# A table of the order of 3662 operations: positions 1075 to 2195 set anew, and 29 maxima tied to VectorE

## The chip, the cores and the metric

The kernel runs on one core of a Trainium2 chip. The metric is the device time of one execution in microseconds (us). The kernel before was run three times: 1040.69, 1041.87 and 1043.01 us, median 1041.87.

## What is computed

Two layers in one kernel, all in fp32:

```python
# linear attention: batch 8, heads 8, 576 positions, head 64, 128 features
proj = x @ w_phi;  proj -= max(abs(proj));  phi = [exp(proj), exp(-proj)]
kv = phi(k).T @ v;  z = sum(phi(k));  num = phi(q) @ kv;  den = phi(q) @ z + 1e-6
x = (num / den) as 4608 tokens x 512
# two dense layers over the tokens
h = x @ w_in                       # 512 -> 2048
g = 0.5 * h * (1 + erf(h / sqrt(2)))
out = g @ w_out                    # 2048 -> 512
```

## The kernel before

**Attention** goes batch by batch (b = 0 to 7), four pairs of heads each. For keys, `k_unit` projects a unit into one PSUM bank ("pp", tile `pk_...`) on TensorE; VectorE takes the row maxima (`mx`) and subtracts them out of the bank into `ek` (or `er` for the last 64 positions, the "rest"); ScalarE makes both exponents; TensorE then multiplies with the values (`kv_...`). `ek` and `er` have two buffers each, one per sign, so the subtraction of a unit writes where the kv product of an earlier unit reads. For queries, `q_front` projects into the same bank (`pq_...`), ScalarE copies it to `pc`, GpSimd takes the maximum over the partitions (`mb`, line 399), VectorE subtracts, ScalarE makes the exponents (`ef`), TensorE forms the numerators (`pn_...`). From batch 3 on the denominators are formed by VectorE (lines 457 and 460) and a sum over the partitions on GpSimd (`db`, line 410); they go through DRAM (`d_d`, `dc`, `r_d`) as reciprocals.

**The dense layers** take 18 blocks of 256 tokens. In blocks 0 to 7 (`block`) there are eight units: "first products" (`up`, into `ph`: 2 x 12 matmuls, each operand split into two fp32r parts `xh`, `xl`), two Gelus on ScalarE (`gh`, and `ph` in place), the difference `gl` on VectorE, and "second products" into `po` (2 x 6 matmuls). Blocks 8 to 17 (`seven`) use seven products of half blocks into `pa` and `pb`; they need sums of the weights `w_out`, which VectorE makes early (`ts`), which are stored in DRAM (`t_d`), and which `fetch_sums` loads into `tw_0` to `tw_7` and back into halves of `w_o0` to `w_o15`. The tw tiles lie where attention's tiles lay, so their loads wait until attention has ended.

**What sets the order.** Each engine runs its instructions in program order. The program is written as a list of operations with their dependencies, and `Plan.order` emits them in the order of the table `ORDER`, 3662 numbers. An operation that comes early for one engine holds up what stands behind it on that engine alone. All DMAs of this kernel but two go through SyncE's queue, which also runs in order. A second table, `TOGETHER`, holds pairs n:m: the GpSimd operation n gets a wait for the VectorE operation that stands just ahead of operation m, so that the reduction begins when VectorE begins m, which reads PSUM:

```python
if o.n in beside:
    ahead[o.n] = last
...
if o.n in together:
    self.tc.add_manual_dep(ins.ins, ahead[together[o.n]].ins.name, ...)
```

A second product's last matmul is cut in two halves of 256 columns where a first product follows (`cut` in `block`).

Of the kernel before, what the change touches and what calls it, by code (L numbers as in the profile page):

```python
# [883 lines left out]
773 1684 1689 1531 1535 807 1532 1680 838 1536 1685 839 822 844 1533 845 846 770 823 808 1741 1537 1539 1538 1540 1541 756 849 1686 1542 809 1690 1543  # L884
857 1544 1742 1545 850 1546 1547 1691 1548 810 1695 1549 811 1687 1692 851 824 840 1803 812 774 1696 919 852 1550 1551 1554 1552 1555 853 1556 1702
813 847 1553 1557 1703 814 825 1693 1697 771 818 1558 1698 1559 1804 854 815 914 1560 796 804 816 1694 826 827 1704 1699 1709 873 915 754 1705 916
1561 828 1564 1700 1565 1701 829 1562 1805 1710 858 1706 830 1566 1567 1716 1806 817 831 1717 917 859 1711 832 1707 1563 819 1708 1712 834 1569 1570
1571 874 893 1568 1574 1572 1809 1718 1575 1573 1719 1713 1576 875 644 1720 1812 860 1723 1577 1714 848 1579 861 1580 923 924 1724 925 1715 1578 876
918 1743 1581 1721 921 1582 920 1584 757 1722 1813 862 1807 926 1585 1583 863 864 855 877 1586 927 1587 865 1589 878 833 931 856 835 1588 1808 820 866
867 928 1590 1725 1726 1047 1591 836 1727 775 870 932 1750 1814 922 1810 1744 879 929 868 1592 933 971 880 1594 1751 1728 871 934 1595 1596 1597 1593  # L890
935 939 1599 1811 1745 1746 881 758 1729 882 894 886 1600 883 1601 936 869 1602 895 1815 1598 887 955 1603 1747 975 1752 1753 1730 1731 1732 1754 896
884 976 897 1604 1733 977 1757 1609 937 1764 898 978 1816 1605 872 900 1610 899 1748 1606 1749 1611 1755 973 1765 979 972 1607 885 1758 1756 901 940
1612 906 902 1759 1608 776 1766 980 1614 1760 1615 1767 907 941 1613 903 1761 1619 1616 1771 1620 1762 1772 956 1621 889 1817 1617 1763 904 1818 957
1618 930 777 1768 1773 905 942 1622 1624 1625 1626 1819 943 1623 1774 1775 1627 1629 944 778 1628 981 1630 908 1778 983 1769 1785 890 1631 945 984 985
1770 1776 1777 986 958 946 974 1779 1632 1633 1634 1635 1048 1636 1820 1639 987 952 988 1637 1640 991 888 1786 1638 1780 947 1781 1641 1782 1881 1787
1792 948 949 1644 1645 1882 938 1783 953 1642 1788 1049 1646 1784 989 1181 1053 1793 959 1050 950 954 960 1789 1821 1790 1647 1054 961 982 1643 1791
1822 1794 1649 990 1650 1651 1648 1795 962 963 1652 1883 1796 1823 964 992 993 1654 1051 891 968 1655 1057 1885 1653 1058 1884 1824 1797 909 1828 1825
1007 994 1052 995 1656 996 1059 1060 1657 1886 1835 997 951 965 1829 969 1798 1055 1887 910 966 1888 1799 1061 1836 1065 1830 1831 1658 1801 1004 1005
1832 1066 1105 998 1062 1889 1950 1826 1827 1833 999 1027 1837 1000 1056 967 1063 1064 1838 1001 1842 892 1002 1843 1067 1834 1068 1006 1069 1839 1844
1070 1109 1800 1106 1840 1951 1107 1845 1952 1953 1849 911 1071 1956 1846 1850 1959 1960 1802 1841 1110 1111 1851 1072 1008 970 1961 1962 1847 1848  # L900
1852 1853 1854 1112 1003 1113 1009 1073 912 1855 1010 1856 1028 1114 1029 1089 1011 1012 1030 1117 1108 1115 1116 1013 1857 1118 1187 1031 1863 1858
1014 1119 1864 1015 1859 1016 1032 1020 1860 1017 1865 1018 1182 1861 1183 1866 1021 1867 1862 1022 1870 1033 1871 1120 1034 1868 1019 1954 1035 1872
1036 1869 1023 1037 1873 1040 1121 1874 1875 1955 1024 1025 1026 1041 1876 1042 1038 1890 1877 1879 1957 1878 1880 1891 1039 1897 1892 1958 1898 1893
1894 1043 1122 1899 1900 1963 1901 1044 1045 1895 1046 1123 1184 1188 1124 1185 1964 1896 1186 1904 1911 1965 1912 1966 1967 1905 2028 1074 1906 1902
1125 1075 2029 1903 1907 1076 1908 1090 1913 1914 2030 1918 1915 1091 1141 1191 1077 2031 1919 1189 1192 1078 1092 1193 1909 1079 1910 1194 1080 1093
1916 1195 1081 1920 1917 1082 1083 1925 1921 1084 1922 1926 1923 1094 1086 1927 1196 1087 1085 1928 1088 1095 1929 1126 1190 1924 1161 1197 1096 1198
1127 1097 1102 1098 1128 1199 1103 1104 1932 1099 1239 1200 1100 1933 1201 1930 1934 1931 1935 1936 1939 1129 1937 1130 1101 1938 1940 1131 1202 1132
1142 2032 1133 1203 1134 1138 1207 1143 1135 1136 1941 1243 1204 1942 1241 1244 1139 2033 1140 1943 1944 1205 1240 1245 1206 1246 1945 1144 1137 1968
1946 2034 1948 1975 1947 1247 1949 2035 1976 1145 1969 2036 1146 1147 2121 1162 1248 1970 1148 1223 1149 1150 2122 1977 1151 1978 1154 1242 1152 1163
1971 1249 1972 1250 1251 2123 1155 1979 1156 1973 1252 2124 1253 1974 1254 1980 1164 2127 1153 1981 1255 1982 1165 1157 1166 1989 1167 1168 1169 1990  # L910
1158 1170 1159 1171 1983 1160 1208 1984 1174 1259 1209 1172 1256 1175 1210 1991 1176 1992 1985 1173 1224 1257 1986 1258 1993 1996 1225 1275 1177 1211
1997 1212 1226 2003 2004 1178 1213 1179 1180 1987 1214 1227 1988 1215 1228 1216 1994 1998 1217 1995 1218 1999 1220 2000 2005 2006 2007 2001 1221 1229
1222 2002 2010 1230 1219 1231 1232 2017 1233 2018 1234 2011 2008 2012 2125 1236 2013 2014 1260 1237 1235 1238 2126 2037 1261 1295 1262 2038 2009 2015
2019 2020 2128 1263 2016 2021 1264 1276 2129 2022 1277 2039 2023 1278 2044 2024 2130 2026 2025 2040 2045 2027 2041 2131 2051 2046 1279 2047 1265 2052
2132 2048 2042 2275 1280 1266 2058 1267 2099 1268 1269 2276 2059 1270 2043 2277 2049 2053 2102 2050 2105 2054 2278 2055 1272 2060 2108 2061 2062 1271
1296 1281 2056 2057 2111 1297 1282 1273 1298 2065 1274 2114 1283 1284 2072 1299 1285 1300 2073 1286 2066 2063 2067 1288 2117 2068 2069 2064 1289 1302
1290 1287 1301 2079 2120 2080 2074 1303 1291 1304 2070 1305 2075 2076 2071 2098 1292 2086 1293 2081 2101 1294 2082 2083 2087 1306 2133 2279 1307 1308
2134 1309 1310 2077 2280 1311 2078 2104 2084 2088 2107 2089 2090 2085 2110 2149 2113 2281 2150 1312 2282 1313 2283 1314 2091 2426 2092 2116 2097 2135
2106 2100 2118 2109 2115 2103 2112 2136 2137 2165 2093 2119 2095 2094 2427 2138 2096 2166 2139 2142 2140 2143 2151 2181 2152 2141 2144 2182 2153 2154
2145 2155 2158 2146 2156 2159 2157 2147 2167 2160 2168 2148 2169 2229 2170 2171 2174 2230 2172 2175 2173 2183 2176 2161 2185 2245 2246 2162 2163 2184  # L920
2186 2164 2187 2197 2190 2188 2191 2189 2213 2192 2214 2198 2177 2199 2430 2201 2178 2179 2200 2202 2180 2203 2193 2206 2204 2194 2207 2215 2195 2205
2216 2208 2196 2284 2428 2217 2218 2219 2300 2222 2220 2223 2231 2221 2301 2224 2233 2431 2316 2429 2317 2285 2209 2225 2432 2210 2226 2232 2433 2234
2211 2235 2238 2227 2236 2434 2247 2212 2228 2248 2332 2237 2239 2577 2240 2249 2241 2250 2242 2251 2254 2243 2252 2580 2255 2253 2244 2286 2256 2257
2287 2288 2258 2261 2262 2265 2259 2289 2266 2581 2263 2290 2264 2260 2267 2333 2268 2269 2270 2271 2348 2272 2273 2582 2291 2274 2293 2292 2294 2302
2349 2295 2303 2304 2305 2364 2306 2309 2307 2583 2310 2308 2365 2318 2311 2320 2380 2381 2296 2312 2297 2313 2319 2321 2298 2322 2325 2314 2323 2326
2334 2299 2315 2335 2328 2324 2327 2329 2336 2330 2337 2331 2338 2396 2341 2339 2342 2340 2350 2343 2344 2351 2352 2345 2353 2346 2354 2357 2347 2355
2435 2358 2366 2367 2356 2360 2359 2368 2361 2369 2362 2370 2373 2363 2371 2436 2374 2372 2382 2375 2383 2384 2376 2385 2377 2386 2389 2378 2387 2390
2388 2379 2451 2391 2392 2393 2394 2395 2452 2397 2467 2398 2578 2399 2400 2401 2483 2402 2405 2403 2484 2406 2437 2579 2438 2404 2408 2407 2439 2409
2412 2413 2416 2410 2440 2417 2414 2584 2441 2415 2411 2418 2468 2419 2420 2421 2422 2499 2423 2424 2442 2425 2444 2443 2445 2453 2500 2446 2454 2455
# [86 lines left out]
```

## Time and profile before

| | us |
|---|---|
| median of three runs | 1041.87 |
| lowest, highest run | 1040.69, 1043.01 |
| the profiled execution | 1041.06 |
| its span, first to last instruction | 1039.3 |
| TensorE busy | 1017.9 |
| VectorE busy | 676.3 |
| ScalarE busy | 605.5 |
| GpSimd busy | 274.8 |

The engines are PE (TensorE, matmuls), PEld (its weight loads, which overlap), DVE (VectorE), ACT (ScalarE), POOL (GpSimd) and SP (SyncE, here the DMA queue). The chain of waits follows the work that ended last back to what released it. "Idle before" is the time an engine sat idle in front of an instruction. [...]

### The profile page before, as it was taken

The numbers are of one execution on the slowest core, as the hardware profiler recorded it, in microseconds if no ns is written. First come the engines' busy times: TensorE is split into PE (matmuls) and PEld (weight loads), VectorE is DVE, ScalarE is ACT, GpSimd is POOL, SyncE is SP. The second block draws the span as 40 slices with busy tenths as digits, with TensorE's granted clock in tenths as the row PEclk, the third lists the DMA queues.
The fourth block names the chain that finished last, engine by engine and source line by source line (L and its number), as shares of the span: only waits on it lengthen the run. The fifth ranks groups of instructions, "written<-read, shape, count | busy, mean of one in ns | idle before, by whom it ended". The sixth has DMA issues, their size and how long they took to land.

```text
span 1039.3 us, 24208 instructions
## 1 busy us (share of the span) xinstructions
PE 1017.9 (98%) x10090; PEld 893.0 (86%) x10090; DVE 676.3 (65%) x1209; ACT 605.5 (58%) x1009; POOL 274.8 (26%) x72
## 2 busy tenths in 40 slices
PE   6979999999999999999999999999999999999998
PEld 5646768788878888887887889999999999999998
DVE  7899999898897875426543424565465546464655
ACT  5989888766877675757764643343343334244433
POOL 1433232544455344416566430000000000000000
PEclk9999999999999999999999999999999999999999
DMA  8765655435335343132321338201201111110000
GB/s 296 228 202 176 204 196 156 144 95 174 116 104 185 116 126 115 58 83 74 92 76 47 94 111 319 46 28 42 55 29 41 42 42 42 42 41 19 24 22 21
DMA packets 87325, 107.10 MB, mean 103 GB/s; under 512 B 29020, under 2 KB 57244, under 8 KB 87216
## 3 DMA queue, kind: packets, MB, share of 16 engines
q1 hardware_dynamic: 86928, 105.30, 32.9%
q8 instruction: 79, 1.29, 0.5%
q10 hardware_dynamic: 288, 0.26, 0.1%
q14 instruction: 30, 0.25, 0.1%
HBM read 75.87 MB, written 29.66 MB: 102 GB/s over the span
## 4 chain that ended last, share of the span: by engine, by line
PE 92%; DVE 2%; ACT 2%; DMA 2%; issue 1%; SPq 0%; DVEq 0%; ACTq 0%
PE ph L220 38%; PE po L220 18%; PE pa L220 10%; PE pb L220 7%; PE pn L220 5%; PE kv L220 5%; PE pq L220 3%; PE pk L220 3%; PE dn L220 1%; PE pn_rest L220 1%; DMA kt<-in_kT_dram 1%; ACT ek L330 1%; DMA qt<-in_qT_dram 1%; DVE ob L261 0%; ACT ef L404 0%
## 5 line engine op out<-in xcount | busy, mean ns | idle before, releaser
L220 PE MATMUL ph<-xh,w_i 128*128 128x256 f32 x2304 | 417.6, 278 | 0.0
L220 PEld LDWEIGHTS ph<-xh,w_i 128*128 128x128 f32 x2304 | 357.3, 188 | 9.1 <-issue 3.8
L220 PE MATMUL ph<-xl,w_i 128*128 128x256 f32 x1152 | 318.6, 277 | 0.0
L220 PEld LDWEIGHTS ph<-xl,w_i 128*128 128x128 f32 x1152 | 216.4, 188 | 0.2
L399 POOL PARTITION_ALL_REDUCE mb<-pc x36 | 119.6, 3321 | 205.8 <-ACT pc L255 112.4
L220 PE MATMUL po<-w_o,gh 128*128 128x512 f32 (+1 forms) x518 | 161.9, 395 | 0.0
L410 POOL PARTITION_ALL_REDUCE db<-pc x20 | 124.4, 6221 | 90.1 <-DVE pc L460 82.0
L261 DVE TENSOR_TENSOR sg<-ga 128x256 f32<-128x256 f32 (+1 forms) x240 | 84.5, 376 | 63.2 <-ACT ga L699 59.9
L220 PEld LDWEIGHTS po<-w_o,gh 128*128 128x128 f32 x518 | 91.8, 188 | 27.4 <-issue 4.7
L220 PE MATMUL pa<-w_o,oh 128*128 128x256 f32 x640 | 112.9, 276 | 0.2 <-DVE ob L261 0.2
L220 PE MATMUL po<-w_o,gl 128*128 128x512 f32 (+1 forms) x296 | 101.1, 363 | 0.0
L699 ACT ACTIVATE ga<-ph 128x512 f32<-128x512 f32 x80 | 47.8, 598 | 90.3 <-PE ph L220 62.4
L261 DVE TENSOR_TENSOR gl<-ph,gh 128x512 fp32r<-128x512 f32 x64 | 43.7, 685 | 84.5 <-ACT ph L610 84.4
L220 PEld LDWEIGHTS pa<-w_o,oh 128*128 128x128 f32 x640 | 96.5, 188 | 0.4 <-DVE ob L261 0.4
L220 PE MATMUL pa<-w_o,ol 128*128 128x256 f32 x320 | 88.4, 276 | 0.0
L261 DVE TENSOR_TENSOR ul<-sg,uh 128x384 fp32r<-128x384 f32 x80 | 44.6, 558 | 67.0 <-ACT uh L255 65.7
L220 PE MATMUL pb<-tw,uh 128*128 128x256 f32 x464 | 83.3, 277 | 0.7 <-DVE ob L261 0.5
L330 ACT ACTIVATE ek<-ek 128x1024 f32<-128x1024 f32 x64 | 67.6, 1057 | 12.6 <-DVE ek L261 10.7
L609 ACT ACTIVATE gh<-ph 128x512 fp32r<-128x512 f32 x64 | 38.2, 598 | 58.8 <-PE ph L220 31.5
L404 ACT ACTIVATE ef<-pc 128x1024 f32<-128x1024 f32 (+1 forms) x72 | 68.1, 972 | 6.8 <-DVE pc L261 6.3
L220 PE MATMUL pn<-ef,kvn 128*64 128x512 f32 (+1 forms) x288 | 65.4, 575 | 5.8 <-ACT kvn L255 3.4
L220 PEld LDWEIGHTS pb<-tw,uh 128*128 128x128 f32 x464 | 70.0, 188 | 1.1 <-DVE ob L261 1.1
(94 smaller groups left out, 1611.2 us busy)
## 6 DMA issues: line engine op xcount, KB each, us to landing
vt<-in_va_dram SPq DMA_DIRECT2D x32, 325.0 KB
t_d<-ts SPq DMA_DIRECT2D x40, 256.0 KB
out_dram<-ob SPq DMA_DIRECT2D x34, 256.0 KB
kt<-in_kT_dram SPq DMA_DIRECT2D x32, 256.0 KB
raw_i<-in_w_in_dram SPq DMA_DIRECT2D x16, 512.0 KB
raw_o<-in_w_out_dram SPq DMA_DIRECT2D x16, 512.0 KB
qt<-in_qT_dram SPq DMA_DIRECT2D x28, 256.0 KB
x_d<-xo SPq DMA_DIRECT2D x28, 256.0 KB
```

Source lines behind the costliest of these rows:

```text
L220: return tc.keep_in_program_order(nc.tensor.matmul(*a, **kw))
L261: op(eng, cost, lambda: e.tensor_tensor(out=dst(), in0=a(), in1=b(), op=o), r=r, w=w, **kw)
L330: op("act", act(256 * n), lambda s=s: nc.scalar.activation(e[s](), e[1](), AF.Exp, scale=1.0 - 2.0 * s), r=[e[1]], w=[e[s]], table="exp", ...
L399: op("pool", plan.SPENT[most], lambda: nc.gpsimd.partition_all_reduce(mb(), pc(), P, bass_isa.ReduceOp.absmax), r=[pc], w=[mb], port=most, ...
L404: op("act", act(2 * n), lambda s=s: nc.scalar.activation(ef[s](), pc(), AF.Exp, scale=1.0 - 2.0 * s), r=[pc], w=[ef[s]], table="exp", **k())
L410: op("pool", plan.SPENT[total], lambda: nc.gpsimd.partition_all_reduce(db(), pc()[:, :2], P, bass_isa.ReduceOp.add), r=[pc], w=[db], port= ...
L609: op("act", act(2 * TB, True) + 0.016, lambda gh=gh, ph=ph: nc.scalar.activation(gh(), ph(), AF.Gelu), r=[ph], w=[gh], table="gelu", rank= ...
L699: op("act", act(2 * TB, True) + 0.037, lambda ph=ph, ga=ga: nc.scalar.activation(ga(), ph(), AF.Gelu), r=[ph_all], w=[ga], table="gelu", a ...
```

## The change

The positions 1075 to 2195 of `ORDER` are a new arrangement of the same operations; the numbers on either side stand as before. On TensorE the moved operations reach from a first product of block 2 to a second product of block 8. The table `TOGETHER` has 29 pairs where it had 23: the first 18 are kept, and in the stretch of the new order five become eleven. No operation is added or taken out. Of `ORDER` two lines are shown.

```diff
@@ ORDER @@
-773 1684 1689 1531 1535 807 1532 1680 838 1536 1685 839 822 844 1533 845 846 770 823 808 1741 1537 1539 1538 1540 1541 756 849 1686 1542 809 1690 1543
+773 1684 1689 1531 1535 807 1532 1680 838 1536 1685 839 822 844 1533 845 846 770 823 808 1741 1537 1539 1538 1540 1541 756 849 1695 1690 1742 1544
...
@@ TOGETHER @@
-48:15 61:14 74:39 87:424 104:431 117:425 130:469 440:475 453:531 484:540 497:547 514:1335 556:584 569:1349 613:647 630:656 690:708 742:1424 824:850
-860:1713 876:925 896:1754 942:1761
+48:15 61:14 74:39 87:424 104:431 117:425 130:469 440:475 453:531 484:540 497:547 514:1335 556:584 569:1349 613:647 630:656 690:708 742:1424 860:916
+876:1706 896:1727 942:977 1010:1839 1128:1908 1144:1200 1210:1972 1226:1252 1262:1979 1278:2000
```

Three places show how instructions move. In the names the first number is the batch (or the block in `ph`, `po`, `gh`, `gl`, `xh`, `xl`), the last one counts buffers.

TensorE, at the projection of the rest of batch 6's keys (`pk_6_r`), before:

```order
L220 MATMUL pk_6_r_4716<-wst_116,kr_6_4145 128x128 x4
L220 MATMUL pn_5_0_0_4727<-ef_5_0_0_0_4613,kvn_5_0_0_4192 64x512 x2
L220 MATMUL pn_5_0_0_4727<-ef_5_0_0_1_4667,kvn_5_0_0_4192 64x512 x2
L220 MATMUL kv_5_1_1_4732<-vt_5_1_1_4697,er_5_0_3901 64x65 x2
...
L220 MATMUL kv_5_1_1_4732<-vt_5_1_1_4697,ek_5_1_1_1_4671 64x65 x2
L220 MATMUL ph_3_6_4652<-xh_3_3261,w_i0_3_2084 128x256
```

and now:

```order
L220 MATMUL pk_6_r_4777<-wst_116,kr_6_4655 128x128 x4
L220 MATMUL kv_5_1_1_4789<-vt_5_1_1_4560,er_5_0_4016 64x65 x2
...
L220 MATMUL kv_5_1_1_4789<-vt_5_1_1_4560,ek_5_1_1_1_4608 64x65 x2
L220 MATMUL pn_5_0_0_4835<-ef_5_0_0_0_4592,kvn_5_0_0_4218 64x512 x2
L220 MATMUL pn_5_0_0_4835<-ef_5_0_0_1_4598,kvn_5_0_0_4218 64x512 x2
L220 MATMUL pq_5_2_0_4851<-qt_5_2_0_4686,wst_116 128x512 x2
L220 MATMUL ph_4_0_4866<-xh_4_4029,w_i0_0_269 128x256
```

The kv product of batch 5's last unit now stands directly behind `pk_6_r`, the numerators `pn_5_0_0` behind it, and the query projection `pq_5_2_0` directly behind those; before, `pq_5_2_0` stood some 75 rows further down, behind block work.

VectorE at the same place, before:

```order
L261 TENSOR_TENSOR ts_7_2_4819<-ts_7_2_4819 128x256
L261 TENSOR_TENSOR ts_7_1_4724<-ts_7_1_4724 128x256
L325 TENSOR_REDUCE mx_6_r_4834<-pk_6_r_4716 128x4
L261 TENSOR_TENSOR pc_5_1_0_4586<-pc_5_1_0_4586,mb_5_1_0_4694 128x1024
L261 TENSOR_TENSOR er_6_1_4863<-pk_6_r_4716,mx_6_r_4834 128x512
L261 TENSOR_TENSOR gl_3_6_4871<-ph_3_6_4652,gh_3_6_4802 128x512
L261 TENSOR_TENSOR ts_7_2_4819<-ts_7_2_4819 128x256
```

and now:

```order
L261 TENSOR_TENSOR ts_7_1_4773<-ts_7_1_4773 128x256
L325 TENSOR_REDUCE mx_6_r_4784<-pk_6_r_4777 128x4
L261 TENSOR_TENSOR ts_7_0_4768<-ts_7_0_4768 128x256 x2
L525 TENSOR_SCALAR dc_4_0_4787<-dc_4_0_4787 128x32
L261 TENSOR_TENSOR gl_3_6_4843<-ph_3_6_4667,gh_3_6_4745 128x512
L261 TENSOR_TENSOR er_6_1_4845<-pk_6_r_4777,mx_6_r_4784 128x512
L261 TENSOR_TENSOR ts_7_1_4773<-ts_7_1_4773 128x256
```

Between the maxima `mx_6_r` and the subtraction into `er_6_1`, which empties the bank, there was one step; now there are two steps of the sums of the weights, a step of the reciprocals and the difference `gl_3_6`.

SyncE's queue, where the sums of the weights are fetched, before:

```order
L671 DMA w_o11_2053<-t_d3_3588 128x2x256
L671 DMA w_o12_2377<-t_d4_3915 128x2x256
L671 DMA w_o13_2388<-t_d5_4093 128x2x256
L527 DMA r_d7_1_7455<-dc_7_1_7394 128x4
L572 DMA xr_10_7463<-x_d4_0_0_4096 128x256
L670 DMA tw_0_7492<-t_d0_2562 128x1536
L671 DMA w_o14_2444<-t_d6_4526 128x2x256
L670 DMA tw_3_7496<-t_d3_3588 128x1536
L670 DMA tw_1_7498<-t_d1_2926 128x1536
L670 DMA tw_7_7500<-t_d7_4791 128x1536
L670 DMA tw_4_7502<-t_d4_3915 128x1536
L670 DMA tw_6_7504<-t_d6_4526 128x1536
```

and now:

```order
L527 DMA r_d7_1_7401<-dc_7_1_7369 128x4
L527 DMA r_d7_0_7416<-dc_7_0_7237 128x32
L671 DMA w_o9_1938<-t_d1_2926 128x2x256
L575 DMA xh_9_7477<-r_d4_0_5103 64x4x256
L670 DMA tw_1_7504<-t_d1_2926 128x1536
L575 DMA xh_9_7477<-r_d4_0_5103 64x4x256
L670 DMA tw_0_7520<-t_d0_2562 128x1536
L671 DMA w_o8_1831<-t_d0_2562 128x2x256
L670 DMA tw_5_7528<-t_d5_4166 128x1536
L670 DMA tw_3_7530<-t_d3_3588 128x1536
L672 DMA w_o6_1458<-t_d6_4477 128x2x256
L670 DMA tw_4_7574<-t_d4_3946 128x1536
```

The stores of the reciprocals (`r_d7_1`, line 527) stood behind four loads into `w_o`; now they stand ahead of them. `w_o8`, which was loaded earlier in the queue, now stands behind `tw_1` and `tw_0`, and the other loads into `w_o` among the `tw`.

## Rows read from the trace of the kernel before

**Rows 1.** The profile's page: busy time of the engines, the chain's shares by engine.

```profile
PE 1017.9 (98%) x10090; PEld 893.0 (86%) x10090; DVE 676.3 (65%) x1209; ACT 605.5 (58%) x1009; POOL 274.8 (26%) x72
...
PE 92%; DVE 2%; ACT 2%; DMA 2%; issue 1%; SPq 0%; DVEq 0%; ACTq 0%
```

**Rows 2.** Busy time by stretch: stretch, its length, each engine's busy us (count), PEclk, DMA.

```profile
266.85:629.68 362.83, 362.83 (x3311) 298.50 (x3310) 209.32 (x281) 234.55 (x322) 173.74 (x39) 1.00 0.34 101
629.68:1039.30 409.62, 404.55 (x3553) 403.66 (x3551) 227.12 (x584) 160.54 (x361) 0.00 (x0) 1.00 0.17 52
```

**Rows 3.** Timeline of TensorE, 176 to 205 us: start, length, what [idle before].

```profile
176.57 1.16 PE L220 MATMUL pk<-wst,kt 64*128 64x128 f32 x16 [0.56 <-ACT pc L255]
...
204.41 1.13 PE L220 MATMUL pq<-qt,wst 64*128 64x512 f32 x4 [1.15 <-issue]
```

**Rows 4.** The chain of waits, 300 to 345 us: start, length, what.

```profile
310.56 2.48 PE kv L220 x80
313.04 1.72 PE pn L220 x8
...
319.05 2.75 PE po L220 x12
...
322.43 1.87 PE pn L220 x8
324.30 2.33 PE kv L220 x80
...
327.72 2.93 PE ph L220 x24
...
334.78 2.72 PE ph L220 x24
...
339.94 1.08 PE pn_rest L220 x32
```

**Rows 5.** The chain of waits, whole span: two pieces of 48 matmuls of first products.

```profile
446.10 5.65 PE ph L220 x48
...
457.20 5.44 PE ph L220 x48
```

**Rows 6.** Costliest groups on VectorE, 265 to 640 us.

```profile
L261 DVE TENSOR_TENSOR gl<-ph,gh 128x512 fp32r<-128x512 f32 x46 | 31.5, 687 | 81.8 <-ACT ph L610 81.8
...
L261 DVE TENSOR_TENSOR ek<-pk,mx 128x1024 f32<-128x1024 f32 x13 | 15.8, 1219 | 0.8 <-PE kv L220 0.5
...
L325 DVE TENSOR_REDUCE mx_r<-pk_r 128x4 f32<-128x512 f32 x3 | 2.1, 687 | 2.3 <-PE pk_r L220 2.3
L261 DVE TENSOR_TENSOR er<-pk_r,mx_r 128x512 f32<-128x512 f32 x3 | 2.0, 676 | 0.0
...
L525 DVE TENSOR_SCALAR dc<-dc 128x32 f32<-128x32 f32 x4 | 1.4, 350 | 1.6 <-DMA dc<-d_d 1.6
```

**Rows 7.** Timelines of VectorE and GpSimd: steps beside reductions.

```profile
269.48 1.60 DVE L261 TENSOR_TENSOR ts<-ts 128x256 fp32r<-128x256 f32 x1
...
287.76 0.41 DVE L261 TENSOR_TENSOR ts<-ts 128x256 fp32r<-128x256 f32 x1
...
289.47 4.64 DVE L261 TENSOR_TENSOR ts<-ts 128x256 f32<-128x256 f32 x1
...
268.62 3.54 POOL L399 PARTITION_ALL_REDUCE mb<-pc  x1 [5.89 <-DVE ts L261]
...
288.99 6.42 POOL L410 PARTITION_ALL_REDUCE db<-pc  x1 [3.02 <-DVE pc L460]
```

**Rows 8.** Hand-over, 604 to 645 us: SyncE's queue, GpSimd, TensorE, and busy time by stretch.

```profile
628.70 0.32 SPq L670 DMA_DIRECT2D tw<-t_d  x1
...
609.25 3.23 POOL L410 PARTITION_ALL_REDUCE db_rest<-un_rest  x1 [4.70 <-DVE un_rest L261]
...
635.33 0.40 PE L220 MATMUL pa<-w_o,oh 128*128 128x256 f32 x2
...
630.00:635.00 5.00, 5.00 (x45) 5.00 (x44) 3.53 (x11) 3.42 (x9) 0.00 (x0) 1.00 0.93 362
```

170 rows, old and new, of the table ORDER are left out of this document.

## The prediction

> **What bounds the kernel now.** I read the page first: TensorE is busy 1017.9 us, 98% of the span, and it holds 92% of the chain that ended last [rows 1]. The next question is whether the stretch that the change touches has any idle time to give back. The first moved TensorE operation stands at 266.85 us, the last that changes place by more than one block at about 629.68 us. [...] The two waits that TensorE still had since 75 us, 0.56 and 1.15 us, lie at 176.57 and 204.41 us, ahead of it [rows 3]. So nothing waits on the path where the order is changed: TensorE's own work is the path there, and a better order of VectorE, ScalarE or GpSimd saves nothing unless TensorE's work itself gets shorter. Behind the stretch the order is as it was, and TensorE is the bound again (404.55 of 409.62 us) [rows 2]. What is gained or lost inside is therefore kept to the end.
>
> **Part 1: TensorE's own work.** The same matmuls run, but some pairs of neighbours cost less. The chain of waits gives the prices. [...] A kv product next to a numerator product is cheaper than apart: kv 2.48 then pn 1.72 is 4.20, pn 1.87 then kv 2.33 is 4.20, and each by itself 2.48 + 1.87 = 4.35 [rows 4]; 0.15 us a neighbourhood. In the order of TensorE I count 33 islands in this stretch before and 30 now (3 x 0.21 = 0.63 us less), and 9 neighbourhoods of kv and pn before, 12 now (3 x 0.15 = 0.45 less). Block work alternates more often between first and second products (105 times against 70), which I cost at nothing: second products between first ones run at 2.75 us a pair [rows 4], next to the 2.72 of first products. Sum of part 1: **-1.08 us**.
>
> There is a second, smaller item. Some pieces of 48 matmuls take 5.65 us where others take 5.44, with no wait named [rows 5]; there are four such (446.10, 511.98, 577.03, 629.84), 0.84 us together. The trace does not say why. An order in which all of them vanish gains 0.84; I take none of it and keep it for the low end.
>
> **Part 2: waits that could arise.** The places where TensorE comes close to another engine decide the upper side. Projections of keys and queries share one PSUM bank ("pp"). A key projection keeps that bank until VectorE has written er or ek out of it, and er and ek have two buffers, so this write must wait for the kv product of the unit before. Before, a query projection followed that kv product at a distance: kv_6_0_1 and pq_5_3_0 had a key projection and four block operations between them, at half of 2.75 each [rows 4] over 5.5 us. Now there are five places where a kv product, VectorE's write and the query projection follow each other closely:
> - pq_6_0_0 behind kv_6_1_1, with only pn_5_rest between: 1.08 us of TensorE work [rows 4] for er, 0.68 us [rows 6]. 0.40 us is left.
> - pq_7_0_0 behind kv_7_1_0, with one first product after attention between (half of 2.72 and 0.21, 1.57) for ek, 1.22 [rows 6]. 0.35 left.
> - pq_5_3_0 behind kv_6_0_1 and pq_6_rest behind kv_7_0_1, each with a numerator product between, 1.87 for ek, 1.22. 0.65 left.
> - pq_5_2_0 behind kv_5_1_1: from the end of pk_6_r TensorE has 4.20 us of work (kv and pn); VectorE has mx_r 0.69, two ts of 0.41, dc 0.35, gl 0.69 and er 0.68 in front of or in it [rows 6, 7], 3.23 us. 0.97 left.
> The hand-over from engine to engine has no row here. All five fit by their rows, with little to spare at two. I charge those two 0.21 us each, the price of the unexplained pieces [rows 5], as the row nearest to a matmul that starts with its operand just there: +0.42. The bounds are 0 (they fit) and one full hold of VectorE, below.
>
> **Part 3: the maxima that wait.** 29 maxima of GpSimd now start with a chosen VectorE operation instead of 23; inside the stretch it is 11 instead of 5. While GpSimd reduces, VectorE loses time: a ts step of 0.41 us took 4.64 beside a sum of 6.42, and one took 1.60 beside a maximum of 3.54 [rows 7]. Six maxima placed better spare VectorE up to 6 x 1.2 = 7 us. The cover is complete (VectorE was idle 362.83 - 209.32 = 153 us in the stretch [rows 2]), so this is worth nothing on the path. What is queued behind a maximum that waits is the subtraction from pc, the exponents and a pn product, which stands 12 us or more of TensorE work behind its pq: cost nothing. ScalarE has four table loads fewer (78 rows before, 74 now), hidden too: ScalarE was idle 128 us there.
>
> **Part 4: the queue of SyncE at the hand-over.** The four sums of weights that the last ten blocks read were fetched early before: 14 of 16 w_o pieces were in the queue ahead of tw_0, and the eight tw followed in one run. Now ten w_o pieces stand among the tw, and w_o8, which the first product of block 8 reads, stands behind tw_1 and tw_0. These fetches wait for the end of attention. Before, the first tw was issued at 628.70, and the first pa product ran at 635.33 without waiting [rows 8]. Ahead of w_o8 there are now two tw of 0.79 MB (128 x 1536 fp32); with its own 0.26 that is 1.83 MB, at the 362 GB/s of that stretch [rows 8] 5.1 us. But pn_7_rest stands 11 TensorE operations earlier (some 15 us), and with it the sum db_7_rest (609.25 before [rows 8]), the reciprocals and the stores. I expect the first tw some 10 us earlier than 628.70, and cost the part at nothing.
>
> **Sum.** -1.08 + 0.42 = -0.66 us. The profiled execution took 1041.06 us (span 1039.3 and 1.8 around it) and would take 1040.4; the median of the three runs shown, 1041.87, lies 0.8 above it, so I forecast **1041.2 us**. Measurement tells apart about 0.2%, 2.08 us: this is no change.
>
> **Rivals.**
> 1. *Slower: a hold of VectorE in front of the bank's release.* If a sum on GpSimd starts while VectorE still has a step between the kv product and er or ek, that step takes 4.64 instead of 0.41 us [rows 7], 4.23 more, and TensorE stands at the query projection for 4.23 minus the 0.35 to 0.97 left: 3.3 to 3.9 us a place. It decides from the first such place: -1.08 + 3.3 = +2.2 to +2.8, 1044.1 to 1044.7 us; with two places 1048. For it: at pq_5_2_0 five VectorE steps stand between, and db_5_0_0 is due just then. Against it: at the other four er or ek stands directly behind mx or has one step between, and VectorE met such holds before without TensorE waiting once in 362.83 us. [...] Chance of this rival **0.15**.
> 2. *Slower: block 8 waits for its sums.* If attention ended no earlier than before, w_o8 would land at 628.70 + 5.1 = 633.8 plus a latency that no row separates, and the first pa, which now has one first product less in front of it and comes 1.1 us earlier, would be due at 632.9: a wait of 0.9 us to about 3. Against it stands the earlier pn_7_rest. 1042 to 1044 us; chance of over 2.08 us **0.04**.
> 3. *Faster by more than 2.08 us.* Part 1 and all four unexplained pieces give -1.08 - 0.84 = -1.92, 1039.95 us. Even this stays short; it needs a saving that no row shows. Chance **0.08**.
> 4. *The maxima do nothing.* If the new waits change no start at all, VectorE keeps its holds, and the end stays the same, since it is covered: 1041.2. This is in the forecast.
>
> **How the numbers follow.** Forecast (within 0.2%) 0.73, rivals 1 and 2 together 0.19, rival 3 0.08. The range goes from 1039.3 (the low bound 1039.95 less 0.6 for the spread of medians, half of the 1.18 between the lowest run, 1040.69, and the median) to 1044.7 (one full hold). That leaves out two holds and more, about 0.1, and a few in a hundred below.
>
> **What would show it.** Right: in the stretch from the first moved operation to the first pa product TensorE has still no wait, the stretch is about 1 us shorter, kv and pn neighbours take 4.20, and the first tw is issued well before 628.7. VectorE's ts steps have a lower mean. Wrong: idle time of TensorE before pq (named after VectorE's er or ek) of 0.5 us or more, or before pa (named after a w_o or tw transfer), or a gain from a shorter matmul pitch that these rows do not have.

## The result and the profile after

The changed kernel took 1047.94 us in the median of six runs (1045.79 to 1049.58) beside 1042.33 for the kernel before; the ratio is 1.0058 with a 95% interval of 1.0044 to 1.0072, so it is 4.6 to 7.5 us slower. A second measurement gave 1.0047 (1.0028 to 1.0065). The forecast was 1041.2 us, no change, with a range from 1039.3 to 1044.7: it is wrong.

The page of the changed kernel, with span, busy times and the chain's shares:

```profile
span 1045.3 us, 24228 instructions
...
PE 1018.9 (97%) x10106; PEld 894.7 (86%) x10106; DVE 697.6 (67%) x1209; ACT 598.5 (57%) x1005; POOL 277.3 (27%) x72
...
PE 88%; DVE 4%; ACT 3%; issue 2%; DMA 1%; SPq 1%; POOL 0%; DVEq 0%; ACTq 0%
```

VectorE is busy 21.3 us longer than before with the same 1209 instructions (697.6 against 676.3 in [rows 1]), and TensorE's share of the chain has fallen from 92 to 88%. The path now goes through VectorE more than before. The busy time by stretch says where; this row is the moved stretch of the changed kernel, to be read against the first of [rows 2]:

```profile
266.85:636.00 369.15, 364.80 (x3354) 301.06 (x3351) 227.57 (x282) 229.22 (x322) 175.92 (x39) 1.00 0.34 102
```

TensorE is idle for 369.15 - 364.80 = 4.35 us where it had no idle time before. To compare the kernels exactly, I take one measure throughout: the time from one operation of TensorE that stands ahead of every moved one (the kv product at 263.27 us before, number 180 in TensorE's order, and at 264.46 now) to one behind them (the first product of block 8 at 645.62 before, number 452, and at 651.14 now). It is called the stretch: **382.35 us before, 386.68 now, +4.33**. Of the other 1.7 us between the two profiles, 1.19 lie ahead of it and 0.50 behind, where both kernels run the same order. The waits of TensorE from 240 to 1000 us (kind: us in all, times, longest) name the idle time:

```profile
PE po L220 <- DVE gl L261: 3.7, 2, 2.0
PE kv L220 <- ACT kvn L255: 0.6, 1, 0.6
PE pb L220 <- DVE ob L261: 0.5, 1, 0.5
PE pa L220 <- DVE ob L261: 0.2, 1, 0.2
```

The last two kinds stand in the kernel before too. New are two waits of second products on VectorE's `gl`, 2.04 and 1.69 us, and one of a kv product on ScalarE's copy `kvn`, 0.61: together 4.34.

**The first place.** The timeline of TensorE in the changed kernel, around 364 us (start, length, what, idle before and its releaser):

```profile
362.17 0.62 PE L220 MATMUL po<-w_o,gh 128*128 128x512 f32 x2
...
362.86 0.62 PE L220 MATMUL po<-w_o,gh 128*128 128x512 f32 x2
365.52 0.50 PE L220 MATMUL po<-w_o,gl 128*128 128x512 f32 x1 [2.04 <-DVE gl L261]
365.86 0.63 PE L220 MATMUL po<-w_o,gh 128*128 128x512 f32 x2
```

The timeline of VectorE at the same place:

```profile
358.04 1.21 DVE L261 TENSOR_TENSOR xl<-xr,xh 128x1024 fp32r<-128x1024 f32 x1
359.17 0.68 DVE L261 TENSOR_TENSOR ts<-w_o,w_o 128x512 f32<-128x512 f32 x1
359.89 4.98 DVE L261 TENSOR_TENSOR ts<-ts 128x256 f32<-128x256 f32 x2
364.79 0.68 DVE L261 TENSOR_TENSOR gl<-ph,gh 128x512 fp32r<-128x512 f32 x1
```

That of ScalarE, whose second Gelu makes the input of `gl`:

```profile
361.46 0.59 ACT L610 ACTIVATE ph<-ph 128x512 f32<-128x512 f32 x1
```

And that of GpSimd:

```profile
357.94 7.89 POOL L410 PARTITION_ALL_REDUCE db<-pc  x1 [11.40 <-DVE pc L460]
```

The sum db_5_0_0 runs from 357.94. Two steps `ts` with 0.4 us of work each take 4.98 us beside it. Behind them in VectorE's queue stands gl_3_5. ScalarE had its input ready at 362.05, TensorE came to the second product at 362.86 and to its first matmul with `gl` 0.6 us later, and `gl` began at 364.79, 2.74 us after its input was ready. TensorE's own work covered 0.70 us of that; the rest is the wait of 2.04. The kernel before had the same hold of the same length, beside the same sum (364.52 to 371.01). Its timeline of VectorE:

```profile
362.42 0.69 DVE L261 TENSOR_TENSOR gl<-ph,gh 128x512 fp32r<-128x512 f32 x1 [1.59 <-ACT ph L610]
...
365.07 4.98 DVE L261 TENSOR_TENSOR ts<-ts 128x256 f32<-128x256 f32 x2
```

And its timeline of TensorE:

```profile
368.97 0.63 PE L220 MATMUL po<-w_o,gh 128*128 128x512 f32 x2
```

There gl_3_5 (362.42) stood ahead of the held steps, and the second product that reads it came at 368.97. The hold cost nothing.

**The second place.** The timeline of TensorE around 581 us:

```profile
579.83 0.62 PE L220 MATMUL po<-w_o,gh 128*128 128x512 f32 x2
582.14 0.50 PE L220 MATMUL po<-w_o,gl 128*128 128x512 f32 x1 [1.69 <-DVE gl L261]
582.48 0.62 PE L220 MATMUL po<-w_o,gh 128*128 128x512 f32 x2
```

The timeline of VectorE there:

```profile
575.93 5.57 DVE L261 TENSOR_TENSOR pc<-pc,mb 128x1024 f32<-128x1024 f32 x1 [0.85 <-POOL mb L399]
581.41 0.68 DVE L261 TENSOR_TENSOR gl<-ph,gh 128x512 fp32r<-128x512 f32 x1
```

That of ScalarE:

```profile
576.75 0.59 ACT L610 ACTIVATE ph<-ph 128x512 f32<-128x512 f32 x1
```

And that of GpSimd:

```profile
571.90 3.99 POOL L399 PARTITION_ALL_REDUCE mb<-pc  x1 [4.54 <-DVE pc L457]
575.80 6.19 POOL L410 PARTITION_ALL_REDUCE db<-pc  x1
```

The maximum ends at 575.9; its end releases two things at once, the subtraction from pc_7_3_0 on VectorE and the sum db_7_2_0 behind it on GpSimd. The subtraction takes 5.57 us (1.23 alone), and gl_6_7, whose input was ready at 577.34, stands behind it. In the kernel before, gl_6_7 stood well ahead of that subtraction (571.89 against 579.87 us), and the sum came after it (585.69).

**The third place** is a chain on ScalarE, here the chain of waits from 304.75 to 314.7 us (start, length, what):

```profile
304.75 1.28 ACT L404
...
306.04 2.01 ACT ef L404 x2
...
310.58 0.96 ACT ek L330
...
311.83 0.28 ACT kvn L255
...
312.15 2.55 PE kv L220 x80
```

The kv product needs its PSUM bank emptied, and the copy `kvn_4_1_1` that does this stands behind a table load, two exponents `ef`, the exponents of `ek` and `er`, and casts. They started late because ScalarE had stood idle for 4.22 us until a `ts` step was done, which took 2.29 us (from 301.96) beside a maximum of 3.84, where the same step at 308.21, beside none, took 0.43.

### The profile page after: what moved, and what is told of

Its sections match the earlier page's. It is cut to its first block, busy times and chain, and to the rows that moved or that the text cites. A ratio compares the mean times of both kernels' runs of the same rounds, so it can differ in the third digit from the quotient of the medians.

```text
span 1045.3 us, 24228 instructions
## 1 busy us (share of the span) xinstructions
PE 1018.9 (97%) x10106; PEld 894.7 (86%) x10106; DVE 697.6 (67%) x1209; ACT 598.5 (57%) x1005; POOL 277.3 (27%) x72
## 4 chain that ended last, share of the span: by engine, by line
PE 88%; DVE 4%; ACT 3%; issue 2%; DMA 1%; SPq 1%; POOL 0%; DVEq 0%; ACTq 0%
PE ph L220 36%; PE po L220 16%; PE pa L220 10%; PE pb L220 7%; PE kv L220 6%; PE pn L220 5%; PE pq L220 3%; PE pk L220 3%; PE dn L220 1%; PE pn_rest L220 1%; ACT ef L404 1%; DMA raw_o<-in_w_out_dram 1%; DMA qt<-in_qT_dram 1%; DVE ts L261 1%; DVE pc L261 1%
## 5 line engine op out<-in xcount | busy, mean ns | idle before, releaser
L220 PE MATMUL ph<-xh,w_i 128*128 128x256 f32 x2304 | 422.1, 278 | 0.0
L399 POOL PARTITION_ALL_REDUCE mb<-pc x36 | 122.1, 3390 | 183.6 <-ACT pc L255 44.8
L220 PEld LDWEIGHTS po<-w_o,gl 128*128 128x128 f32 x312 | 58.7, 188 | 16.9 <-DVE gl L261 4.6
L255 ACT CAST uh<-sg 128x384 fp32r<-128x384 f32 x80 | 40.9, 512 | 53.2 <-PE pb L220 25.9
```

What stands on the lines that cost most here:

```text
L220: return tc.keep_in_program_order(nc.tensor.matmul(*a, **kw))
L255: op(eng, cost, lambda: nc.scalar.copy(out=dst(), in_=src()), r=r, w=w, **kw)
L399: op("pool", plan.SPENT[most], lambda: nc.gpsimd.partition_all_reduce(mb(), pc(), P, bass_isa.ReduceOp.absmax), r=[pc], w=[mb], port=most, ...
```

## The experiments

All versions below differ in the two tables alone; the diffs show pieces of the tables' lines. Measured is the stretch of the profiled execution, and where there are timed runs the ratio to the kernel before with its interval. The kernel before against itself shows how far each can be trusted.

> The kernel before against itself: a ratio of 1.000 with its interval over it, and a stretch of 382.35 us within 0.1. It shows how much the part ahead of the stretch differs between runs of one program (single profiles so far reach the first moved operation between 262.5 and 267.4 us).

Measured: ratio 1.0000 (0.9987 to 1.0014), and the stretch 382.35 us again, to the hundredth. The stretch began 2.74 us later than in the profile shown ahead of the prediction (266.01 against 263.27). So the part ahead of the stretch wanders by some us from run to run, and the stretch of this kernel doesn't: tenths of a us can be read in it from one profile, apart from one thing that the last run shows.

**The pairs, or the order?**

```diff
@@ TOGETHER @@
-860:916 876:1706 896:1727 942:977 1010:1839 1128:1908 1144:1200 1210:1972 1226:1252 1262:1979 1278:2000
```

> The new order, with only the 18 pairs that both tables share (the 11 inside the stretch are gone). Theory (two sums of GpSimd hold VectorE in front of gl_3_5 and gl_6_7; sums are in no pair): both waits of TensorE on gl stay, 3.5 to 4 us together, and the time stays 4 to 7 us above the kernel before. Rival (the new pairs shifted the reductions into the wrong places): the two waits go, and the time is within 2 us of the kernel before.

Measured: stretch 386.66 us, the same three waits (3.7 and 0.6 us), 1047.27 us, ratio 1.0052 (1.0037 to 1.0068). In this order the eleven pairs make no difference: the loss is in the order. The other way round, the order of before with the 29 pairs:

> The order of before with the 29 pairs of the change. Theory (order alone costs): no new wait of TensorE in the stretch, time within 1 us of the kernel before. Rival (the pairs cost): 2 us or more above it, with waits of TensorE that the kernel before does not have.

Measured: stretch 383.16 us (+0.81), ratio 1.0011 (0.9998 to 1.0024), which can't be told from no change. Yet it has one wait that I had not expected, 0.53 us of a first product on `gl`. The timeline of VectorE in that version, around 270 us:

```profile
268.89 3.20 DVE L261 TENSOR_TENSOR xl<-xr,xh 128x1024 fp32r<-128x1024 f32 x1
...
274.43 0.68 DVE L261 TENSOR_TENSOR gl<-ph,gh 128x512 fp32r<-128x512 f32 x1
```

And that of GpSimd:

```profile
268.54 3.84 POOL L399 PARTITION_ALL_REDUCE mb<-pc  x1 [3.79 <-DVE pc L261]
```

The old table's pair 824:850 held this maximum back until VectorE was past the step `xl` (it is the one released by `ts` in [rows 7]), which took 1.22 us; in the new table the pair is gone, the maximum starts behind the subtraction, and `xl` takes 3.20. It is the same hold again, on a smaller scale.

**Is it the hold in front of gl?** Two moves in VectorE's order put `gl` first at the two places:

```diff
@@ ORDER, first place @@
-1629 1777 1630 987 1626 907 1780 1781 1627 1782 1783
+1629 1777 987 1626 907 1780 1781 1782 1630 1627 1783
@@ ORDER, second place @@
-1269 1279 2019 2020 2038 2021 1280
+1269 2019 2020 2038 2021 1279 1280
```

> The changed kernel, with two places of VectorE's order mended: gl_3_5 ahead of two steps of the sums of the weights, gl_6_7 ahead of the subtraction from pc_7_3_0. Theory: the two waits of TensorE on gl (2.04 and 1.69 us) are gone, the steps that now stand behind gl are held instead at no cost, and the time falls by 3 to 4 us against the changed kernel's 5.6 above the kernel before, so to 1.5 to 2.5 us above it. Rival (gl itself is held beside a sum): waits of 1.5 us or more on gl stay, and the time stays 4 us or more above.

Measured: stretch 382.25 us, 4.43 less than the changed kernel, more than the 3.73 of the waits by themselves; the ratio is 0.9995 (0.9982 to 1.0008). Most of the difference is in how idle time is counted: where nothing waits, a matmul starts before the row of the one ahead of it ends (the one at 362.62 us before the end, at 362.79, of the row that starts at 362.17). From start to start, the three matmuls at the two waits take 3.00 us (362.86 to 365.86) and 2.65 (579.83 to 582.48), and 0.69 where nothing waits (362.17 to 362.86): 2.31 + 1.96 = 4.27 us. The waits of TensorE from 240 to 1000 us that are left:

```profile
PE kv L220 <- ACT kvn L255: 0.6, 1, 0.6
PE pb L220 <- DVE ob L261: 0.5, 1, 0.5
PE pa L220 <- DVE ob L261: 0.2, 1, 0.2
```

One place at a time:

> The changed kernel with only the first place mended: gl_3_5 ahead of two steps of the sums of the weights. If the two waits are independent, the one of 2.04 us goes, the one of 1.69 stays, and the stretch is 384.2 to 384.7 us. If the first wait gave the second place its slack (TensorE late, VectorE not), the second wait grows to 2.5 us or more.

> The changed kernel with only the second place mended: gl_6_7 ahead of the subtraction from pc_7_3_0. The wait of 2.04 us stays, that of 1.69 goes, and the stretch is 384.5 to 385.0 us; together with the run that mends only the first place the two gains add up to that of both, 4.43 us, within 0.3.

Measured with the first place alone: only the wait of 1.68 us is left of the two, stretch 384.20, a gain of 2.48 us, at the edge of what was expected. With the second alone: the wait of 2.04 is left, but the stretch is 386.26, a gain of 0.42 where 1.7 to 2.2 were expected. The miss has a cause of its own, the clock, and is taken up below; without its 1.54 us the gain is 1.96, and 2.48 + 1.96 = 4.44 is what both gave together.

**Is it the sum, or VectorE's order by itself?** Here VectorE's order stays, and the two sums wait for `gl`:

```diff
@@ ORDER, the sum db_7_2_0 behind the next step of VectorE @@
-2023 1270 2044
+2023 2044
...
-1282
+1282 1270
@@ TOGETHER @@
+950:1632 1270:1282
```

> The changed kernel with VectorE's order as it is, but the two sums of GpSimd, db_5_0_0 and db_7_2_0, wait until VectorE has done gl_3_5 and gl_6_7 (two pairs more in the table; db_7_2_0 is emitted a little later for it). Theory (the sum's start is what holds VectorE): the two steps of ts and the subtraction from pc_7_3_0 take their own 0.8 and 1.2 us, gl is done in time, and both waits of TensorE on gl go: the stretch from op 180 to op 452 of TensorE falls by 3.5 to 4.5 us, to 382.2 to 383.2, as in the run that moved gl. Rival (VectorE's order alone is at fault, the steps ahead of gl are long by themselves): the waits stay and the stretch stays at 386 us or more.

Measured: stretch 382.26 us, no wait on `gl`, ratio 0.9994 (0.9983 to 1.0006). The timeline of VectorE at the first place of this version:

```profile
358.47 0.76 DVE L261 TENSOR_TENSOR ts<-ts 128x256 f32<-128x256 f32 x2
360.66 0.69 DVE L261 TENSOR_TENSOR gl<-ph,gh 128x512 fp32r<-128x512 f32 x1 [1.43 <-ACT ph L610]
...
361.60 5.03 DVE L261 TENSOR_TENSOR ts<-w_o,w_o 128x512 f32<-128x512 f32 x1
```

And that of GpSimd:

```profile
361.51 6.15 POOL L410 PARTITION_ALL_REDUCE db<-pc  x1 [16.39 <-DVE gl L261]
```

The two `ts` steps take 0.76 us with the sum out of their way; gl_3_5 starts when ScalarE is ready, and the sum, which now begins behind it at 361.51, holds another step for 5.03 us, behind which nothing is late. At the second place, in VectorE's timeline of the same version, the subtraction takes 1.23 us:

```profile
572.07 1.23 DVE L261 TENSOR_TENSOR pc<-pc,mb 128x1024 f32<-128x1024 f32 x1 [0.85 <-POOL mb L399]
573.52 0.69 DVE L261 TENSOR_TENSOR gl<-ph,gh 128x512 fp32r<-128x512 f32 x1 [0.23 <-ACT ph L610]
```

**What does the distance to the second product buy?** One first product of 1.36 us is moved ahead of the waiting second product:

```diff
@@ ORDER @@
-1782 1783 1792 1631 1786
+1782 1786 1783 1792 1631
```

> The changed kernel with one operation of TensorE moved: the second half of the first products of unit 6 of block 3, 1.36 us, stands ahead of the second product that reads gl_3_5. Theory (a hold costs what it exceeds the TensorE work between gl's first products and its second product): the wait at this place falls from 2.04 to about 0.7 us, the one on gl_6_7 stays at 1.7, and the stretch falls by 1.2 to 1.5 us, to about 385.3. Rival (the wait is set by the length of the hold alone, or the second product is late for another reason): no fall, or the same wait a little further on.

Measured: the wait at the first place is 0.68 us, 2.04 - 1.36, and the stretch is 385.18. The timeline of TensorE at that place:

```profile
365.14 0.50 PE L220 MATMUL po<-w_o,gl 128*128 128x512 f32 x1 [0.68 <-DVE gl L261]
```

**The third wait too**, with `kvn` ahead of the exponents of `er`:

```diff
@@ ORDER @@
-917 1714 1579 921 1807 1743 1580 1584 918
+917 1714 1579 921 1807 1743 1580 1584 855 918
...
-877 855 866
+877 866
```

> As the run before, and kvn_4_1_1, the copy that releases the bank of kv, moved ahead of the exponents of er_5_1 on ScalarE. Theory: the wait of 0.61 us on kvn goes too; TensorE has no wait in the stretch, and the time is 0.4 to 0.8 us below that of the run with two places mended. If the third wait hid another behind it, TensorE waits at the same kv product for er or ek instead, and the time is that of the run before. What then stays above the kernel before, 1 us or so, would come from ahead of the stretch or behind it.

Measured: stretch 381.67 us, no wait left in it, 1040.24 us against 1042.28, ratio 0.9981 (0.9971 to 0.9990). That is faster than both kernels, but by more than the 0.68 us of the stretch explain, so it was run again:

> The version with three places mended, once more. Its stretch is 0.68 us shorter than that of the kernel before. If only the stretch counts, the ratio is 0.9993, and the 0.9981 of the first time held luck of the part ahead of it; then this ratio's interval reaches 0.9995 or more. If the version is really 2 us faster, the ratio comes out at 0.998 again with an interval below 0.9995.

Measured: stretch 381.80 us, 1041.11 against 1041.57, ratio 0.9993 (0.9981 to 1.0005). What is shown is a stretch 0.55 to 0.68 us shorter than before's; that the program is faster by the 2 us of the first measurement is not.

**The whole change once more:**

> The changed kernel once more, beside the kernel before. Its stretch is 4.33 us longer than that of before. If only the stretch counts, the ratio is 1.0042 and its interval holds that; the 1.0058 of the first time then held luck of the part ahead of the stretch. If the change costs more than its stretch, the ratio is 1.0055 or more again, with an interval above 1.0042.

Measured: 1047.74 us against 1041.73, ratio 1.0047 (1.0028 to 1.0065), which holds 1.0042 and doesn't decide the question. But this profile's stretch is 388.18 us, 1.50 more than the first time, with the same three waits. The busy time in steps of 1 us behind the wait at the first place (PEclk, the share of full speed that the clock of TensorE was granted, is the third number from the end) shows why:

```profile
367.00:368.00 1.00, 1.00 (x5) 0.81 (x6) 0.14 (x1) 0.00 (x0) 1.00 (x2) 0.78 0.73 272
368.00:369.00 1.00, 1.00 (x6) 1.00 (x6) 0.67 (x1) 0.00 (x0) 1.00 (x1) 0.50 0.83 267
...
370.00:371.00 1.00, 1.00 (x7) 1.00 (x7) 0.09 (x1) 0.00 (x0) 0.69 (x1) 0.52 0.03 9
371.00:372.00 1.00, 1.00 (x11) 1.00 (x10) 0.97 (x2) 0.00 (x0) 0.00 (x0) 1.00 0.00 0
```

In the first profile of the same kernel the steps behind that wait all have 1.00:

```profile
366.00:367.00 1.00, 1.00 (x9) 0.91 (x8) 0.02 (x1) 0.00 (x0) 1.00 (x1) 1.00 0.86 297
367.00:368.00 1.00, 1.00 (x11) 1.00 (x10) 1.00 (x1) 0.00 (x0) 1.00 (x1) 1.00 0.44 136
```

After the wait of 2.04 us TensorE was granted a clock of 0.50 for some 3 us, and lost 1.50 us by it. In the version with only the second place mended the same happened at the same wait, for 1.54 us (from the start of the stretch to the next kv product 109.95 us, against 108.41 in the first profile of the changed kernel). One of its slow steps, in the same view:

```profile
366.00:367.00 1.00, 1.00 (x7) 1.00 (x6) 1.00 (x1) 0.00 (x0) 1.00 (x1) 0.50 0.28 77
```

Four profiles have that wait of 2.04 us (the changed kernel twice, without its new pairs, and with the second place mended), and in two of them the clock fell behind it. If half of the runs pay the 1.5 us, which four profiles can't show, the change costs 4.33 + 0.75 = 5.1 us on average. That is an estimate; the medians of the three timed versions with this wait lie 5.0 to 6.0 us above the kernel before.

## Why the prediction was wrong

- **What bounds the kernel** held: TensorE is the path in the stretch, it had no idle time to give back (busy 362.83 of 362.83 us in [rows 2]), and a shorter path could only come from its own work.
- **Part 1** was right in kind and too large: -1.08 us forecast. Its 0.21 us of an island, a run of attention matmuls inside block work, is the difference of two rows of [rows 4]: two first products took 2.93 us at 327.72, behind a key projection, and 2.72 at 334.78, behind a second product. No run shows why they differ. The version without waits has a stretch 0.68 us shorter (0.55 the second time). Added up by neighbours, its trace has the 0.45 of the kv and pn neighbours in full; what took 0.4 of the islands' 0.63 back wasn't tried.
- **Part 2 is the step that failed**, and with it the cover of part 3. It asked which places TensorE comes close to another engine, and listed only the query projections behind `er` and `ek`. None of the five waited, so the 0.42 us charged there was not due: at pq_5_2_0 `er` was done at 376.19 us and the projection ran at 377.07, 0.88 us left where 0.97 were reckoned. The list left out the second products behind `gl` (2.48 and 1.96 us) and the kv product behind `kvn` (0.58, the stretch of 382.25 less 381.67), and part 1 had costed the alternation of first and second products "at nothing" by its duration alone. The alternation also decides how much TensorE work lies between a unit's first products and the second product that reads its `gl`. At gl_3_5 that second product came 7.9 us behind the end of the first products before (361.1 to 369.0), and 4.1 now (358.7 to 362.9); here both this distance and VectorE's order changed, and mending either shortened the wait. At gl_6_7 the time from the ready input to the first matmul that reads `gl` hardly changed (3.4 us before, 571.17 to 574.58; 3.1 now, 577.34 to 580.45). There the wait comes from VectorE's order, which put the held subtraction ahead of `gl`. Less the 0.68 us of part 1, the two places and the third make up the stretch: 4.43 + 0.58 - 0.68 = 4.33.
- **Rival 1** named the right mechanism, a VectorE step held beside a sum of GpSimd, with 3.3 to 3.9 us a place, and even the right sum, db_5_0_0, but put it at the wrong place. It expected this sum at pq_5_2_0, at 377.07 us, where two `ts` steps stand ahead of `er`; the sum had ended at 365.83, and no reduction ran between `mx_6_r` (372.99) and the projection. It met the two `ts` steps ahead of gl_3_5 instead. No `er`, `mx_r`, `ek` or `mx`, which read PSUM, was held from 265 to 640 us: beside a reduction `er` took at most 0.69 us (2 of 3), `mx_r` 0.68 (2 of 3), `ek` 1.23 (5 of 13) and `mx` 1.23 (8 of 13). The groups of VectorE, 265 to 640 us of the changed kernel (count, busy, mean ns), answer to [rows 6]:

```profile
L261 DVE TENSOR_TENSOR gl<-ph,gh 128x512 fp32r<-128x512 f32 x46 | 31.6, 687 | 71.5 <-ACT ph L610 71.5
L261 DVE TENSOR_TENSOR pc<-pc,mb 128x1024 f32<-128x1024 f32 x16 | 28.2, 1764 | 12.0 <-POOL mb L399 12.0
...
L261 DVE TENSOR_TENSOR ek<-pk,mx 128x1024 f32<-128x1024 f32 x13 | 15.9, 1221 | 3.5 <-PE kv L220 3.1
```

The 46 differences `gl` still have a mean of 687 ns and `ek` 1221, though 30 and 5 of them ran beside a reduction (none of the 30 took over 0.69 us), while the subtractions `pc<-pc,mb`, with both operands in SBUF, have risen from 1234 to 1764. So what matters is not whether the waited-for step is held, but whether a step ahead of it in VectorE's queue is. The wait at a place is the delay of `gl` less the slack behind it: 2.04 and 1.69 us, not 3.3 to 3.9, and two places instead of one. `gl`, which has one input in PSUM, took 0.68 to 0.69 us alone and beside a reduction. The two holds were shorter than the sums beside them: 4.22 us (4.98 less 0.76) beside a sum of 7.89 at the first place, and 4.34 (5.57 less 1.23) beside one of 6.19 at the second, where the subtraction's row ends at 581.50, ahead of the sum's at 581.99.
- **Part 3** said that holds lie under complete cover since VectorE was idle 153 us. That was an average over the stretch: the 5 us behind which `gl` stood were not covered. It also saw VectorE spared up to 7 us; from 266.85 to 636 us VectorE was busy 227.57 us where the kernel before had 213.91. The pairs themselves cost nothing in the new order, as forecast (386.66 us without the eleven, 386.68 with them).
- **Part 4** held. The first tw was issued at 622.48 us, 6 us earlier than in [rows 8] (10 were forecast) though TensorE was late by then, and no first product of block 8 waited for its sums:

```profile
622.48 0.47 SPq L670 DMA_DIRECT2D tw<-t_d  x1
```

- **The chances.** The slower end, where the change came out, had 0.19, and the range stopped at one full hold. Two holds stood in the text (1048 us) and were left outside. That 1048 is so near to the measured 1047.94 is luck: it has two places of 3.3 to 3.9 us, and the two that were found cost 2.48 and 1.96, with the third wait and what lies outside the stretch as the rest.

## What to carry to other kernels

When an order is changed, list for every engine-to-engine hand-over the slack between producer and consumer before and after, all kinds of them, and not only the hand-overs that look new: a finer interleaving on the bound engine can shorten the slack, as at the first place (7.9 us before, 4.1 now). A step that is sometimes held must not stand in the queue ahead of one for which the bound engine waits; put the waited-for step first, or let the reduction start behind it, which worked equally well here (a stretch of 382.25 and of 382.26 us). Idle time of an engine over a stretch is no cover for a wait at a point.

## What the runs showed of the hardware

One wait of 2.04 us of TensorE was followed in two of four profiles by some 3 us at a granted clock of 0.50, and cost 1.5 us more there; the waits of 1.69 and 0.68 us were not followed by it in any profile. A hold moves with the sum: delayed until `gl` was done, the sum took the next step of VectorE for 5.03 us, as before it had taken the two ahead of `gl` for 4.98. Not every step beside a sum is held: at the first place `xl` and a `ts` step took their own 1.21 and 0.68 us within the first 1.9 us of the sum's row, and that row is 7.89 us long, where the same sum has 6.49 in the kernel before and 6.15 in the version in which it waits for `gl`. What stays open is why that is so, why the clock fell in some executions only, and how the part ahead of the stretch comes to differ by up to 5 us (262.5 to 267.4) between executions of the same instructions.
